# Local-window attention and two wide products on one core: contexts split straight from PSUM, a reordered head, and q/k blocks of 736 columns

## The chip, the cores and the metric

The kernel runs on one core of one Trainium2 chip. The metric is device time in microseconds (us) of one execution; smaller is better. The engines are TensorE (PE, with its weight loads shown as PEld), VectorE (DVE), ScalarE (ACT), GpSimd (POOL) and SyncE (SP), which here issues all the transfers. Everything is 32-bit floating point. A product of full precision is made of three passes, high by high, high by low and low by high, so each operand exists as a "high" tile and a "low" tile.

## The reference

```python
# 4 batches, 8 heads, 512 local and 32 global positions, head width 64, window 32
s_g   = scale * q_g @ concat(k_g, k_l).T;  out_g = softmax(s_g) @ concat(v_g, v_l)
s_ll  = where(|i - j| <= 32, scale * q_l @ k_l.T, -1e9)
s_l   = concat(scale * q_l @ k_g.T, s_ll); out_l = softmax(s_l) @ concat(v_g, v_l)
x = concat(out_g, out_l) as (2176 tokens, 512)
x = max(x @ w1, x @ w2, x @ w3) @ w_out          # inner width 768
x = softplus(x @ w_in) @ w_out2                  # inner width 2048
```

## The kernel before, in words

The order on each engine is written out by hand: one stream of attention steps (`att_stream`), one stream that turns the weights from their stored 64-bit form into high and low tiles (`dec_stream`, four DVE operations, an ACT copy and a POOL subtraction for each of 24 weight tiles), and loops over the products that step through both.

**Attention.** There are 32 groups k: batch, half of the sequence (hf), pair of heads (pr). A group's block `kq` holds the queries of four blocks of 64 positions (u = 0 to 3) and the keys. `s1` makes the scores of the four query blocks and two heads, eight matmuls of 64 rows and 64 columns of weights each (L142), into the one PSUM tile `ps`, and DVE masks them into `s` and takes the row extremes (L148). `s1e` is the Exp on ACT (L155), `s1f` the reciprocal on DVE and the scaling on POOL, `s2` five transposes into `pw` and `pg` (L211, L212), `s2e` their evictions to `pwt` and `pgt` (L223 and L225 on ACT, L227 on DVE), `s3` the context product `po` (L238, L242), `s3h` and `s3l` its eviction. Iteration k runs `s1(k)`, `s3` of group k-3 and `s2` of group k-2. The scores of the global queries are made by `s1g` (tile `psg`, copied to `gsc`), softmaxed by `gsoft` in three steps (L195; L197; L199 to L201), transposed by `g2` (`pb`, `pa`), and multiplied by `g3` (`pog`, evicted by `g3e`).

**Units.** Eight groups of four make eight units u of 256 columns (288 with the global rows, for odd u). The first product (`up`, tile `pu`, L516 to L518) of unit u reads the context as `xh` and `xl`. For units 0 and 1 `s3h` and `s3l` split `po` from PSUM into them; for units 2 to 7 `s3h` copies `po` to `xo` and sends it to the DRAM tile `xd`, and `load_x` fetches it (`xr`) and splits it. The maximum `m` of three `pu` tiles is split by `split_h` into `hh` and `hl`, which the second product (`down`, tile `pd`, L562 to L564) reads. The PSUM tiles `po`, `pw`, `pg`, `psg`, `pa`, `pb`, `pog`, `pu` and `pd` share five buffers of the pool `pm`.

**The head** is the stretch of iterations k < 12 (`KS`), where attention runs ahead and the products of unit 0 begin at k = 7. Then follow the products of units 0 and 1 (until the last of `w1`, `w2`, `w3` is decoded they use each weight as it comes), `down(0)`, `down(1)`, and so on. From about 160 us on TensorE works nearly without a gap to the end.

Of the kernel before, what the change touches and what calls it, by code (L numbers as in the profile page):

```python
# [21 lines left out]
def body(ctx, tc, kq, vw, vb, qg, w1, w2, w3, w_out, w2_in, w2_out, out):  # L22
# [8 lines left out]
    HLP = 3  # L31
# [16 lines left out]
    mask = const.tile([128, 3, 160], F32, name="mask")  # L48

    def setup():  # L50
        g = nc.gpsimd
        g.memset(mask[:, 0, :], 0.0)
        for hh in range(2):
            m = mask[64 * hh:64 * hh + 64, 0, 0:128]
# [4 lines left out]
        g.memset(mask[0:64, 1, 0:32], NEG)  # L59
        g.memset(mask[64:128, 2, 96:128], NEG)  # L60
# [3 lines left out]
    raw, qgs, vbs = {}, {}, {}  # L64

    def load_kq(k):
# [6 lines left out]
        st[k] = {"q": t[:, 0:256].rearrange("p (u n) -> p u n", n=64), "kT": t[:, 256:896].rearrange("p (u n) -> p u n", n=160)}  # L73
# [17 lines left out]
    xs = {}  # L91
    gs = {}
# [6 lines left out]
    def split_x(u, ks, ns, p):  # L99
        xh, xl = xs[u] if u in xs else new_x(u)  # L100
# [3 lines left out]
    def load_x(u):  # L104
        n = 256 + 32 * (u % 2)
        xh, xl = new_x(u)
        xr = []
        for k in range(4):
            xr.append(hp.tile([128, 288], F32, tag="m", name="xr")[:, 0:n])
            nc.sync.dma_start(out=xr[k], in_=xd[u][:, k, 0:n])  # L110
        yield
        for k in range(4):
            nc.scalar.activation(xh[:, k, 0:n], xr[k], AF.Copy)
            (nc.gpsimd if XLP > u else nc.vector).tensor_tensor(xl[:, k, 0:n], xr[k], xh[:, k, 0:n].bitcast(F32), op=ALU.subtract)
            yield
# [11 lines left out]
    def s1(k, w):  # L127
        b, hf, pr = groups[k]
        g = st[k]
        if w == 0:  # L130
            if k < KL:
                g["s"] = wp.tile([128, 4, 160], F32, tag="w", name="s")
            else:
                g["s"] = at.tile([128, 4, 160], F32, tag="s", name="s", bufs=3)
# [11 lines left out]
        for i in range(2):  # L146
            x = 2 * w + i
            nc.vector.tensor_tensor_reduce(out=s[:, x, :], in0=ps[:, i, :], in1=mask[:, mi, :], scale=-scale, scalar=BIG,  # L148
                                           op0=ALU.add, op1=ALU.min, accum_out=g["nm"][:, x:x + 1])

    def s1e(k, i):
        g = st[k]
        s = g["s"]
        for u in (2 * i, 2 * i + 1):
            nc.scalar.activation(s[:, u, :], s[:, u, :], AF.Exp, scale=-1.0, bias=g["nm"][:, u:u + 1], accum_out=g["sm"][:, u:u + 1])  # L155

    def s1f(k):
# [6 lines left out]
        nc.gpsimd.tensor_tensor(s[:, :, 0:128], s[:, :, 0:128], rs.unsqueeze(2).to_broadcast([128, 4, 128]), op=ALU.mult)  # L164
        nc.gpsimd.tensor_tensor(sg, s[:, :, 128:160], rs.unsqueeze(2).to_broadcast([128, 4, 32]), op=ALU.mult)
        g["sg"] = sg

    def s1g(k):
# [3 lines left out]
        ps = ptile([128, 288], "psg")  # L172
        ks = [st[k - 1]["kT"], g["kT"]]
        r = raw[b, hf, s]
        for j in range(2):
            kk = ks[j].rearrange("p (a c) n -> p a c n", c=2)
            nc.tensor.matmul(ps[64 * j:64 * j + 64, 0:256], lhsT=qgs[b][:, pr - 1 + j, :], rhs=kk[:, :, 0, 0:128], start=True, stop=True)
# [3 lines left out]
        else:  # L181
            for j in range(2):
                nc.tensor.matmul(ps[64 * j:64 * j + 64, 256:288], lhsT=qgs[b][:, pr - 1 + j, :], rhs=ks[j][:, 3, 64:96], start=True, stop=True)
# [20 lines left out]
    def s2(k):  # L204
# [5 lines left out]
        for x in range(4):  # L210
            nc.tensor.transpose(pw[:, 128 * x:128 * x + 128], g["s"][:, x, 0:128], ident)  # L211
# [1199 lines left out]
```

## Time and profile before

| what | value |
|---|---|
| median of 3 runs | 780.06 us (778.52 to 780.24) |
| the profiled execution's own time | 780.84 us |
| its span, first to last instruction | 779.1 us |
| TensorE busy | 750.6 us (96%) |
| VectorE busy | 571.7 us (73%) |
| ScalarE busy | 373.4 us (48%) |
| GpSimd busy | 250.8 us (32%) |
| mean granted TensorE clock | 0.998 |

All times of rows are counted from the span's start. 1.74 us of the execution's time lie outside the span.

### The profile page before, as it was taken

The numbers are of one execution on the slowest core, as the hardware profiler recorded it, in microseconds if no ns is written. First come the engines' busy times: TensorE is split into PE (matmuls) and PEld (weight loads), VectorE is DVE, ScalarE is ACT, GpSimd is POOL, SyncE is SP. The second block draws the span as 40 slices with busy tenths as digits, with TensorE's granted clock in tenths as the row PEclk, the third lists the DMA queues.
The fourth block names the chain that finished last, engine by engine and source line by source line (L and its number), as shares of the span: only waits on it lengthen the run. The fifth ranks groups of instructions, "written<-read, shape, count | busy, mean of one in ns | idle before, by whom it ended". The sixth has DMA issues, their size and how long they took to land.

```text
span 779.1 us, 18128 instructions
## 1 busy us (share of the span) xinstructions
PE 750.6 (96%) x6984; PEld 722.0 (93%) x6984; DVE 571.7 (73%) x1438; ACT 373.4 (48%) x955; POOL 250.8 (32%) x240
## 2 busy tenths in 40 slices
PE   5779999999999999999999999999999999999998
PEld 3669998898999999999999999999999999999998
DVE  5978985677786686693991465544686889999996
ACT  5865445654554652233432455533554444444443
POOL 4544441112211210161960488943872000000000
PEclk9999999999999999999999999999999999999999
DMA  8938225777767746578010455445539923444432
GB/s 332 363 128 312 105 84 184 261 283 248 257 213 250 251 170 203 197 267 295 12 42 28 151 179 200 138 159 185 175 132 370 378 93 109 136 136 135 137 95 82
DMA packets 80742, 145.62 MB, mean 187 GB/s; under 512 B 10128, under 2 KB 45840, under 8 KB 80656
## 3 DMA queue, kind: packets, MB, share of 16 engines
q1 hardware_dynamic: 80656, 144.47, 53.9%
q8 instruction: 55, 0.90, 0.5%
q14 instruction: 31, 0.25, 0.1%
HBM read 98.63 MB, written 45.81 MB: 185 GB/s over the span
## 4 chain that ended last, share of the span: by engine, by line
PE 77%; DVE 8%; DMA 4%; ACT 4%; issue 3%; POOL 3%; SPq 0%; POOLq 0%; ACTq 0%; DVEq 0%
PE pu L516 8%; PE pu L518 8%; PE pu L517 8%; PE z L1216 6%; PE z L1040 6%; PE z L1041 6%; PE z L1039 6%; PE z L1215 6%; PE z L1214 6%; DMA raw<-in_w_dram 3%; PE pog L294 2%; PE ps L142 2%; PE pd L562 2%; PE pd L563 2%; PE po L238 2%
## 5 line engine op out<-in xcount | busy, mean ns | idle before, releaser
L516 PE MATMUL pu<-xh,w 128*128 128x256 f32 (+1 forms) x576 | 169.2, 294 | 0.5 <-DVE m L530 0.5
L518 PE MATMUL pu<-xh,w 128*128 128x256 f32 (+1 forms) x576 | 166.5, 289 | 0.8 <-POOL w L453 0.8
L517 PE MATMUL pu<-xl,w 128*128 128x256 f32 (+1 forms) x576 | 166.7, 289 | 0.0
L1216 PE MATMUL z<-v,oo 128*128 128x256 f32 x480 | 136.8, 285 | 0.5 <-DVE oo L1210 0.4
L1215 PE MATMUL z<-v,oo 128*128 128x256 f32 x480 | 135.6, 282 | 0.0
L1214 PE MATMUL z<-v,oo 128*128 128x256 f32 x480 | 135.1, 282 | 0.0
L1040 PE MATMUL z<-o,wi 128*128 128x272 f32 x448 | 129.0, 288 | 1.6 <-POOL o L652 1.6
L1041 PE MATMUL z<-o,wi 128*128 128x272 f32 x448 | 129.1, 288 | 0.0
L1039 PE MATMUL z<-o,wi 128*128 128x272 f32 x448 | 128.7, 287 | 0.1
L516 PEld LDWEIGHTS pu<-xh,w 128*128 128x128 f32 x576 | 109.2, 190 | 3.4 <-issue 1.5
L518 PEld LDWEIGHTS pu<-xh,w 128*128 128x128 f32 x576 | 108.8, 189 | 1.2 <-POOL w L453 1.2
L517 PEld LDWEIGHTS pu<-xl,w 128*128 128x128 f32 x576 | 109.0, 189 | 0.0
L1209 ACT ACTIVATE oo<-sm 128x640 fp32r<-128x640 f32 (+1 forms) x72 | 49.8, 692 | 93.4 <-DVE sm L1204 87.5
L1216 PEld LDWEIGHTS z<-v,oo 128*128 128x128 f32 x480 | 90.8, 189 | 1.3 <-DVE oo L1210 1.0
L1214 PEld LDWEIGHTS z<-v,oo 128*128 128x128 f32 x480 | 91.3, 190 | 0.1
L1215 PEld LDWEIGHTS z<-v,oo 128*128 128x128 f32 x480 | 90.9, 189 | 0.0
L164 POOL TENSOR_TENSOR s<-s,rs 128x512 f32<-128x512 f32 x32 | 34.5, 1079 | 161.3 <-DVE rs L162 94.4
L1040 PEld LDWEIGHTS z<-o,wi 128*128 128x128 f32 x448 | 84.1, 188 | 2.2 <-POOL o L652 2.2
L1039 PEld LDWEIGHTS z<-o,wi 128*128 128x128 f32 x448 | 84.5, 189 | 0.3 <-DVE h L1061 0.3
L1041 PEld LDWEIGHTS z<-o,wi 128*128 128x128 f32 x448 | 84.2, 188 | 0.0
L1210 DVE TENSOR_TENSOR oo<-sm,oo 128x640 fp32r<-128x640 f32 (+1 forms) x72 | 55.0, 764 | 16.5 <-ACT oo L1209 12.8
L652 POOL TENSOR_TENSOR o<-ot,o 128x544 fp32r<-128x544 f32 x36 | 50.9, 1426 | 45.8 <-DVE h L1082 33.8
(161 smaller groups left out, 1641.8 us busy)
## 6 DMA issues: line engine op xcount, KB each, us to landing
gd<-a SPq DMA_DIRECT2D x32, 544.0 KB, 3.1
gl<-gd SPq DMA_DIRECT2D x32, 512.0 KB, 7.1
kq<-in_kq_dram SPq DMA_DIRECT2D x31, 448.0 KB, 5.9
raw<-in_w_out_dram SPq DMA_DIRECT2D x22, 512.0 KB, 4.6
raw<-in_w_dram SPq DMA_DIRECT2D x18, 512.0 KB, 7.6
vt<-in_vw_dram SPq DMA_DIRECT2D x16, 512.0 KB, 6.5
raw<-in_w_in_dram SPq DMA_DIRECT2D x16, 512.0 KB, 5.3
ot<-od SPq DMA_DIRECT2D x24, 272.0 KB, 3.1
```

The lines of the kernel that those rows point to most:

```text
L516: nc.tensor.matmul(p, lhsT=w[:, 0, k], rhs=xh[:, k, 0:n], start=(k == 0), stop=False)
L517: nc.tensor.matmul(p, lhsT=w[:, 0, k], rhs=xl[:, k, 0:n], start=False, stop=False)
L518: nc.tensor.matmul(p, lhsT=w[:, 1, k], rhs=xh[:, k, 0:n], start=False, stop=(k == 3))
L652: nc.gpsimd.tensor_tensor(w[:, 1], src, w[:, 0].bitcast(F32), op=ALU.subtract)
L1039: nc.tensor.matmul(z, lhsT=w[:, 0, k], rhs=x[:, 0, k], start=st and k == 0, stop=False, skip_group_check=True)
L1040: nc.tensor.matmul(z, lhsT=w[:, 0, k], rhs=x[:, 1, k], start=False, stop=False, skip_group_check=True)
L1041: nc.tensor.matmul(z, lhsT=w[:, 1, k], rhs=x[:, 0, k], start=False, stop=sp and k == 1, skip_group_check=True)
L1209: nc.scalar.activation(oh[:, a:b], src, AF.Copy)
L1210: nc.vector.tensor_tensor(ol[:, a:b], src, oh[:, a:b].bitcast(F32), op=ALU.subtract)
L1214: nc.tensor.matmul(p, lhsT=oh[:, a], rhs=w[:, 0], start=st, stop=False, skip_group_check=True)
L1215: nc.tensor.matmul(p, lhsT=oh[:, a], rhs=w[:, 1], start=False, stop=False, skip_group_check=True)
L1216: nc.tensor.matmul(p, lhsT=ol[:, a], rhs=w[:, 0], start=False, stop=sp, skip_group_check=True)
```

## The change

It has four parts.

1. `kq` blocks have 736 columns for 896 (368 KB for 448 KB). Instead of four copies of 128 keys and 32 global keys, a block holds global keys, a run of 192 keys, global keys, another run of 192, global keys; query blocks u = 0 and 1 read two stretches of 160 columns that share a run, as u = 2 and 3 do. With this a query block's half of the PSUM rows is chosen by u // 2 and its columns by u % 2 (before: the other way round), and mask, `s`, `po` and `pwt` are indexed to match.
2. Context tiles of units 2 and 3 are also split straight from PSUM when the tiles `xh`, `xl` of the unit two before have been read by all of its `up` products (`here`, `freed`, `direct`); `load_x` fetches only the parts that were not.
3. In the head: `flush()` evicts the pending `pu` before each `s1`; in iterations with a `g2` the evictions `s3h` and `s2e` come before the Exp; the global softmax begins one iteration earlier; `psg` and `pog` share one PSUM buffer in odd iterations.
4. The low halves `hl` of unit 0 are all made on POOL (before: three of six; the others on DVE); the split of unit 1's `m` comes after all of `down(0)`, and 6 steps of attention (before: 4) stand between that and `down(1)`.

```diff
-    HLP = 3
+    HLP = 6
...
-        t = ld.tile([128, 896], F32, tag="kq", name="kq", bufs=5)
+        t = ld.tile([128, 736], F32, tag="kq", name="kq", bufs=5)
         if k == 0:
-            nc.sync.dma_start(out=t[:, 0:576], in_=kq[k][:, 0:576])
-            nc.sync.dma_start(out=t[:, 576:896], in_=kq[k][:, 576:896])
+            nc.sync.dma_start(out=t[:, 0:512], in_=kq[k][:, 0:512])
+            nc.sync.dma_start(out=t[:, 512:736], in_=kq[k][:, 512:736])
...
     def load_x(u):
-        n = 256 + 32 * (u % 2)
-        xh, xl = new_x(u)
+        xh, xl = xs[u] if u in xs else new_x(u)
+        parts = []
+        for k in range(4):
+            x = [(u, k) not in direct, u % 2 and (u, "g" + str(k // 2)) not in direct]
+            if any(x):
+                parts.append((k, slice(0 if x[0] else 256, 288 if x[1] else 256)))
...
             for u in range(4):
                 for i in range(2):
                     h = slice(64 * i, 64 * i + 64)
-                    r0, c0 = 64 * (u % 2), 160 * (u // 2)
-                    nc.tensor.matmul(g["ps"][r0:r0 + 64, i, c0:c0 + 160], lhsT=g["q"][h, u, :], rhs=g["kT"][h, u, :], start=True, stop=True)
+                    r0, c0, k0 = 64 * (u // 2), 160 * (u % 2), (0, 96, 224, 320)[u]
+                    nc.tensor.matmul(g["ps"][r0:r0 + 64, i, c0:c0 + 160], lhsT=g["q"][h, u, :], rhs=g["kT"][h, k0:k0 + 160], start=True, stop=True)
...
+    def here(u, x):
+        if u not in xs and u - 2 in freed:
+            new_x(u)
+        if u in xs:
+            direct.add((u, x))
+        return u in xs
...
-        if 2 * b + hf < 2:
-            if hf not in xs:
-                new_x(hf)
-            nc.scalar.activation(xs[hf][0][:, pr:pr + 1, 0:256], po.unsqueeze(1), AF.Copy)
+        if here(2 * b + hf, pr):
+            nc.scalar.activation(xs[2 * b + hf][0][:, pr:pr + 1, 0:256], po.unsqueeze(1), AF.Copy)
             return
...
             if k < KS:
+                if True:
+                    flush()
                 s1(k, 0)
                 s1(k, 1)
...
+                joint = ptile([128, 352], "psg") if late and k % 2 == 1 else None
                 for c in late:
-                    g3(*c)
+                    g3(*c, None if joint is None else joint[:, 288:352])
+                if gq and q3 is not None:
+                    s3h(q3)
+                if gq and q2 is not None:
+                    s2e(q2)
                 s1e(k, 0)
                 s1e(k, 1)
-                if q3 is not None:
+                if not (gq) and q3 is not None:
                     s3h(q3)
...
                 if gq:
                     g2(*gq)
-                elif gpend:
+                if gpend:
                     soft = gsoft()
                     next(soft)
...
-        if by_row:
-            for f in range(6):
-                split_h(u + 1, f)
         for j in range(2):
             o = hp.tile([128, 288], F32, tag="m", name="o")[:, 0:n]
...
-        AS = 4
+        AS = 6
...
             if u == 0:
+                for f in range(6):
...
+                    split_h(1, f)
                 for _ in range(AS):
                     step()
```

Three places in the order of the engines, before and after. ACT in iteration k = 8 of the head: `s` is the score tile of group 8 (Exp), `pg` and `pw` are the transposes of group 6, `pu` the first product of unit 0, and `pa` one of the transposes of the global softmax. Before:

```order
L452 ACTIVATE w<-tmp 128x512
L155 ACTIVATE s,sm<-s,nm 128x160 x4
L252 ACTIVATE xh<-po 128x256
L223 ACTIVATE pgt<-pg 128x128
L225 ACTIVATE pwt<-pw 128x512
L527 ACTIVATE m<-pu 128x256
L458 ACTIVATE tmp<-raw 128x512
L282 ACTIVATE gt<-pa 128x384
```

After:

```order
L476 ACTIVATE w<-tmp 128x512
L551 ACTIVATE m<-pu 128x256
L267 ACTIVATE xh<-po 128x256
L233 ACTIVATE pgt<-pg 128x128
L235 ACTIVATE pwt<-pw 128x512
L161 ACTIVATE s,sm<-s,nm 128x160 x4
L482 ACTIVATE tmp<-raw 128x512
L207 ACTIVATE gsc,gsm<-gsc,gnm 128x544
L297 ACTIVATE gt<-pa 128x384
```

The four evictions of PSUM tiles stand ahead of the Exp now, and the Exp of the second global softmax (`gsc`) has come into this iteration from the next.

DVE in iterations 9 and 10: the end of that global softmax. Before, it stands in iteration 10, right behind that iteration's scores (`rs` is the reciprocal of group 9) and ahead of the eviction of `pb`, its transpose:

```order
L161 TENSOR_SCALAR rs<-sm 128x4
L162 RECIPROCAL rs<-rs 128x4
L199 TENSOR_SCALAR gsm<-gsm 128x1
L200 RECIPROCAL gsm<-gsm 128x1
L201 TENSOR_SCALAR gsc<-gsc,gsm 128x544
L530 TENSOR_TENSOR m<-m,pu 128x256
L472 TENSOR_SCALAR tmp<-tmp 128x512
```

After, it stands in iteration 9, ahead of the eviction of `pw`:

```order
L167 TENSOR_SCALAR rs<-sm 128x4
L168 RECIPROCAL rs<-rs 128x4
L209 TENSOR_SCALAR gsm<-gsm 128x1
L210 RECIPROCAL gsm<-gsm 128x1
L211 TENSOR_SCALAR gsc<-gsc,gsm 128x544
L237 COPY pwt<-pw 128x512
L508 SCALAR_TENSOR_TENSOR tmp<-raw,t_724 128x512
```

It moved one iteration ahead, and the eviction of `pw` waits behind it.

DVE at the end of `down(0)`: `hl` are the six low halves of unit 1, `s,nm<-ps` the masking of a group's scores (four pieces, each with a second row for its extremes), `tmp` words of the next weights. Before, the splits stand ahead of the first of the four pieces:

```order
L227 COPY pwt<-pw 128x512
L161 TENSOR_SCALAR rs<-sm 128x4
L162 RECIPROCAL rs<-rs 128x4
L632 TENSOR_SCALAR tmp<-tmp 128x512
L634 TENSOR_SCALAR tmp<-tmp 128x512
L548 TENSOR_TENSOR hl<-m,hh 128x288 x6
L148 ISA s,nm<-ps,mask 128x160
```

After, the same four pieces follow the two operations on `tmp`, and these rows come behind the last piece:

```order
L154 ISA s,nm<-ps,mask 128x160
L154 ISA nm 128x1
L278 TENSOR_TENSOR xl<-po,xh 128x256
L661 SCALAR_TENSOR_TENSOR tmp<-raw,tmp 128x512
L665 SCALAR_TENSOR_TENSOR tmp<-raw,tmp 128x512
L205 TENSOR_REDUCE gnm<-gsc 128x1
L653 TENSOR_SCALAR tmp<-tmp 128x512
L655 TENSOR_SCALAR tmp<-tmp 128x512
L572 TENSOR_TENSOR hl<-m,hh 128x288 x6
```

The six splits moved behind the scores and behind five operations on words and the global softmax, and a split of a context tile (`xl<-po`) came in.

## Rows read from the trace of the kernel before

**Rows 1.** The page, busy time of each engine (us, share of the span, instructions).
```profile
PE 750.6 (96%) x6984; PEld 722.0 (93%) x6984; DVE 571.7 (73%) x1438; ACT 373.4 (48%) x955; POOL 250.8 (32%) x240
```

**Rows 2.** Waits of TensorE over the whole span: total us, times, longest.
```profile
PE ps L142 <- DMA kq<-in_kq_dram: 5.5, 2, 3.8
PE po L238 <- ACT pgt L223: 3.8, 5, 1.0
...
PE pog L294 <- DVE pwt L227: 1.3, 2, 0.7
...
PE pu L518 <- POOL w L453: 0.8, 2, 0.6
```

**Rows 3.** Busy time of each engine in four stretches.
```profile
core 0: us, PE busy (x) PEld busy (x) DVE busy (x) ACT busy (x) POOL busy (x), PEclk, DMA share, GB/s
...
10.40:17.20 6.80, 6.80 (x68) 4.71 (x69) 6.00 (x25) 4.75 (x19) 3.23 (x5) 1.00 1.03 412
...
12.90:41.00 28.10, 21.28 (x309) 16.46 (x309) 26.62 (x102) 23.05 (x87) 16.71 (x19) 0.99 0.91 352
41.00:67.00 26.00, 23.41 (x305) 20.25 (x305) 20.09 (x64) 15.97 (x52) 10.89 (x13) 0.95 0.48 169
67.70:111.00 43.30, 42.47 (x350) 41.67 (x350) 39.91 (x77) 19.96 (x40) 18.86 (x15) 1.00 0.39 148
```

**Rows 4.** Timeline, TensorE's wait for the first global queries.
```profile
10.40 1.12 PE L177 MATMUL psg<-kq,qg 128*64 128x256 f32 x4 [2.23 <-DMA qg<-in_qg_dram]
```

**Rows 5.** Timeline of ACT and PE in iteration 8, and a stretch's busy times and clock.
```profile
38.74 0.43 ACT L155 ACTIVATE s<-s,nm 128x160 f32<-128x160 f32 x1 [0.93 <-DVE nm L148]
...
40.67 0.26 ACT L223 ACTIVATE pgt<-pg 128x128 f32<-128x128 f32 x1
...
40.98 1.12 PE L275 MATMUL pa<-ident,gsc 128*128 128x128 f32 x4 [2.76 <-ACT pgt L223]
...
40.38:43.79 3.41, 2.81 (x13) 2.78 (x14) 2.13 (x6) 3.33 (x10) 1.34 (x3) 0.50 0.00 0
```

**Rows 6.** Timeline of DVE and PE in iteration 10.
```profile
56.63 1.15 DVE L201 TENSOR_SCALAR gsc<-gsc,gsm 128x544 f32<-128x544 f32 x1
...
57.92 0.29 PE L272 MATMUL pb<-ident,gsc 128*96 128x128 f32 x1 [1.24 <-DVE gsc L201]
```

**Rows 7.** Timeline of the decoding stretch: low halves on DVE and POOL, PE's last wait.
```profile
83.52 0.43 DVE L548 TENSOR_TENSOR hl<-m,hh 128x256 fp32r<-128x256 f32 x1 [0.49 <-ACT hh L545]
...
65.49 0.73 POOL L548 TENSOR_TENSOR hl<-m,hh 128x256 fp32r<-128x256 f32 x1 [0.31 <-ACT hh L545]
...
95.49 0.39 PE L518 MATMUL pu<-xh,w 128*128 128x256 f32 x1 [0.58 <-POOL w L453]
```

**Rows 8.** Timeline of DVE and PE at the end of `down(0)`.
```profile
128.09 2.29 DVE L548 TENSOR_TENSOR hl<-m,hh 128x288 fp32r<-128x288 f32 x6
130.30 0.32 DVE L148 CUSTOM_DVE_ANT_0 s<-ps,mask 128x160 f32<-128x160 f32 x1
...
131.46 0.37 PE L142 MATMUL ps<-kq 64*64 64x160 f32 x4 [1.73 <-issue]
```

**Rows 9.** Timeline of ACT and PE in `down(1)`.
```profile
142.40 0.75 ACT L113 ACTIVATE xh<-xr 128x256 fp32r<-128x256 f32 x2 [3.17 <-DMA xr<-xd]
...
145.04 0.39 ACT L186 ACTIVATE gsc<-psg 128x288 f32<-128x288 f32 x1
...
145.48 0.41 PE L562 MATMUL pd<-hh,w 128*128 128x288 f32 x1 [1.58 <-ACT gsc L186]
```

**Rows 10.** Score matmuls (L142) of iteration 9: records; PE, PEld records in a stretch.
```profile
L142 PE MATMUL ps<-kq x16: 296/296/347, 45.7 to 46.2; 64*64 64x160 f32 x16
...
45.66:45.71 0.05, 0.03 (x4) 0.03 (x4) 1.00 0.00 0
...
45.86:45.89 0.03, 0.03 (x8) 0.03 (x8) 1.00 0.00 0
...
45.99:46.03 0.04, 0.04 (x12) 0.04 (x8) 1.00 0.00 0
```

More of the change, by code (lines that the diff above doesn't have):

```diff
@@ L47, in body @@
     ident = const.tile([128, 128], F32, name="ident")
-    mask = const.tile([128, 3, 160], F32, name="mask")
+    mask = const.tile([128, 3, 192], F32, name="mask")
     def setup():
@@ L99, in split_x @@
     def split_x(u, ks, ns, p):
-        xh, xl = xs[u] if u in xs else new_x(u)
+        xh, xl = xs[u]
         nc.scalar.activation(xh[:, ks, ns], p, AF.Copy)
@@ L104, in load_x @@
     def load_x(u):
-        n = 256 + 32 * (u % 2)
-        xh, xl = new_x(u)
+        xh, xl = xs[u] if u in xs else new_x(u)
[4 more added lines that the diff above has]
+                parts.append((k, slice(0 if x[0] else 256, 288 if x[1] else 256)))
         xr = []
-        for k in range(4):
-            xr.append(hp.tile([128, 288], F32, tag="m", name="xr")[:, 0:n])
-            nc.sync.dma_start(out=xr[k], in_=xd[u][:, k, 0:n])
+        for k, c in parts:
+            xr.append(hp.tile([128, 288], F32, tag="m", name="xr")[:, 0:c.stop - c.start])
+            nc.sync.dma_start(out=xr[-1], in_=xd[u][:, k, c])
         yield
-        for k in range(4):
-            nc.scalar.activation(xh[:, k, 0:n], xr[k], AF.Copy)
-            (nc.gpsimd if XLP > u else nc.vector).tensor_tensor(xl[:, k, 0:n], xr[k], xh[:, k, 0:n].bitcast(F32), op=ALU.subtract)
+        for (k, c), r in zip(parts, xr):
+            nc.scalar.activation(xh[:, k, c], r, AF.Copy)
+            nc.vector.tensor_tensor(xl[:, k, c], r, xh[:, k, c].bitcast(F32), op=ALU.subtract)
             yield
@@ L171, in s1g @@
         g = st[k]
-        ps = ptile([128, 288], "psg")
+        ps = ptile([128, 288], "psg") if joint is None else joint
         ks = [st[k - 1]["kT"], g["kT"]]
@@ L175, in s1g @@
         for j in range(2):
[L176 to L177 removed]
+            kk = ks[j][:, 32:480].rearrange("p (c n) -> p c n", n=224)[:, :, 0:128]
+            nc.tensor.matmul(ps[64 * j:64 * j + 64, 0:256], lhsT=qgs[b][:, pr - 1 + j, :], rhs=kk, start=True, stop=True)
         if hf == 0:
@@ L182, in s1g @@
             for j in range(2):
-                nc.tensor.matmul(ps[64 * j:64 * j + 64, 256:288], lhsT=qgs[b][:, pr - 1 + j, :], rhs=ks[j][:, 3, 64:96], start=True, stop=True)
+                nc.tensor.matmul(ps[64 * j:64 * j + 64, 256:288], lhsT=qgs[b][:, pr - 1 + j, :], rhs=ks[j][:, 384:416], start=True, stop=True)
             t = gs[b, s]["t"]
@@ L237, in s3 @@
             for i in range(2):
-                nc.tensor.matmul(po[64 * i:64 * i + 64, 2 * w:2 * w + 2, :], lhsT=vbs[b, s][:, e, w, 64 * i:64 * i + 64], rhs=g["pgt"],
+                nc.tensor.matmul(po[64 * i:64 * i + 64, w:w + 3:2, :], lhsT=vbs[b, s][:, e, w, 64 * i:64 * i + 64], rhs=g["pgt"],
                                  start=(w == 0), stop=False, skip_group_check=True)
@@ L288, in g3 @@
         vs = [(v0, 0, 128), (v0, 2, 128), (v1, 0, 128), (v1, 2, 64), (v1, 3, 96)]
-        po = ptile([128, 2, 32], "pog")
+        if joint is None:
+            joint = ptile([128, 64], "pog")
+        po = joint.rearrange("p (a n) -> p a n", n=32)
         for e in range(2):
@@ L350, in att_stream @@
                 next(soft, None)
-                if q2 is not None:
+                if not (gq) and q2 is not None:
                     s2e(q2)
@@ L363, in att_stream @@
                 if k % 2 == 1:
-                    s1g(k)
+                    s1g(k, None if joint is None else joint[:, 0:288])
                 for c in late:
@@ L867, in slot @@
             pos[u] += 1
+            if pos[u] == 18:
+                freed.add(u)
         def ready(u):
@@ L956, in body @@
             ldx = itertools.chain.from_iterable(load_x(v) for v in loads_x)
-            if loads_x:
-                next(ldx)
+            next(ldx, None)
             for c in range(4):
@@ L971, in body @@
             if u == 0:
+                for f in range(6):
+                    if f >= 1:
+                        for _ in range(0):
+                            step()
+                    split_h(1, f)
                 for _ in range(AS):
```

55 lines of the change are left out of this document (31 added, 24 removed).

## Prediction

> **What bounds the kernel now.** I read the page first: TensorE is busy for 750.6 us of a span of 779.1 [rows 1]. The change neither adds nor takes away a matmul, so there are 28.5 us to win, TensorE's idle time, and what it runs at half clock. The waits of TensorE say where that idle time is: nearly all of it is ahead of 150 us, in the start (5.5 us for q/k blocks, 3.8 us for evictions) and then in single waits [rows 2]. Three stretches of the busy times tell what is behind them [rows 3]. From 12.9 to 41 us DVE is the bound (26.6 of 28.1 us busy) and TensorE waits at every group. From 41 to 67 us neither is (TensorE 23.4 and DVE 20.1 of 26): the engines wait for each other in turn. From 67.7 to 111 us TensorE is busy for 42.5 of 43.3 us, and DVE, which decodes the weights that TensorE reads, for 39.9. So a gain made before 67 us arrives only if the decoding moves forward with it; this is the point to check. Behind 150 us TensorE has no idle time worth counting until the second half, which the change does not touch, so what is won before then stays won.
>
> **The change part by part.** *Smaller q/k blocks.* A block is 160 of 896 columns smaller, 80 KB. Up to 17 us the DMA is full (share 1.03, 412 GB/s [rows 3]) and TensorE and DVE wait for landings, the last time TensorE at 10.40 us for the global queries [rows 4]. Ahead of these three blocks are in the queue, 240 KB, 0.6 us at that rate; by 17 us five, 1.0 us. I take 0.8 us; the bounds are 0 (the waits end with something else) and nine blocks, 1.8 us. All later saving of bytes lies under a TensorE that does not wait for DMA, and is worth nothing here.
>
> *Evictions ahead of the Exp.* In iteration 8 the transposes `pa` wait 2.76 us for ACT's `pgt` [rows 5]. ACT is at the Exp of group 8, for which it waited until 38.74 us, and the eviction of group 6 stands behind that. After the change the order on ACT is `m`, `xh`, `pgt`, `pwt`, Exp: all four have their inputs before 38.2 us, so `pa` follows `pb` directly. The wait goes but for 0.1 us: 2.7. Behind the wait the clock was granted at 0.50, the lower of the two levels, from 40.38 to 43.79 us; TensorE was busy for 2.81 us of it [rows 5], work of 1.4 us at the full clock. Without the gap it should not fall: 1.3. What is late next is the Exp, by the 1.2 us that four evictions take; it feeds the transposes of group 8 in iteration 10, some 10 us later.
>
> *Softmax one iteration earlier, shared buffer.* `pb` waits 1.24 us for the end of the second global softmax on DVE [rows 6], which takes 1.15 us there. It moves to iteration 9, where DVE has room (5.9 us idle in this stretch), so the wait is gone: 1.2. It now stands ahead of the eviction of `pw`, which is then 1.5 us later; `pog` waited for just that one, 1.3 us in two places [rows 2]. With the shared buffer `pog` takes one that a `pu` left and that `flush()` empties before the scores: 1.3, bounds 0 and 1.3. These four terms make 6.5 us by 67 us, on TensorE.
>
> *Does the decoding follow?* DVE's place in the order is tied to TensorE by the scores and by `m`. Laying the new DVE order over the durations of the old rows from iteration 8 on, I find DVE's scores of iteration 11 some 6 us earlier too, with the same decoding behind it, because it fills the 5.9 us in which it was idle. The weights' transfers follow, since SP issues them behind `pog` and `psg`. *Low halves on POOL:* between 67.7 us and the last weight of the first product DVE makes two of them, alike, 0.43 us each with a wait of 0.49 us for ACT in front [rows 7]: 1.8 us less for the decoding. On POOL one takes 0.73 us, in gaps between its weights; `down(0)` needs them only 15 us later. So the decoding gains more than TensorE, and its waits for weights, the last at 95.49 us, 0.8 us in all [rows 2, 7], go: 0.8.
>
> *Split of unit 1 moved.* At 131.46 us TensorE waits 1.73 us for the buffer of the scores, because DVE does six `hl` (2.29 us) ahead of reading the scores [rows 8]. Behind the scores they are out of its way: 1.7. But then they come some 4 us later, since five more operations stand ahead of them, while `down(1)` reads the first of them just behind two groups' worth of attention matmuls. TensorE may wait for `hl` there instead, between 0 and the whole 1.7; the splits then run at 0.38 us each (2.29 for six), faster than `down(1)` uses them, so only the first can be late. I put 0.3 on it: 1.4.
>
> *Unit 2 from PSUM.* ACT stands 3.17 us for the landing of `xr`, and its eviction of `gsc` comes late for `pd`, 1.58 us [rows 9]. Of the four fetches one is left, of a part stored long before. The wait goes: 1.5. For unit 3 no wait was there: 0.
>
> The sum is 0.8 + 2.7 + 1.3 + 1.2 + 1.3 + 0.8 + 1.4 + 1.5 = 11.0 us. 780.84 us for the execution profiled gives 769.8; it lies 0.8 above the median of the runs, so I forecast **769.5**.
>
> *The score matmuls.* They are the part whose price the trace does not show. The eight matmuls of a group leave 16 records, two each, and four of them run at a time: four begin within 0.05 us, four more by 45.89 us and four more by 46.03, a round each 0.135 us [rows 10]. These are the four places that the loop visits in turn (two heads by two halves of the PSUM rows). After the change the halves are chosen by u // 2, so four matmuls in a row go to two places, then four to the other two. If TensorE looks far enough ahead, all four places work at once as before: 0. If not, a group takes up to 8 rounds instead of 4: four pairs of matmuls with two records each, 7 if only the change of halves overlaps. 24 of 32 groups (k from 8 on) lie where TensorE is dense, so each further round costs 24 x 0.135 = 3.25 us, and the bounds are 0 and 13. I take 0, because a far look is already needed: the fourth matmul starts ahead of the first one's second record.
>
> The Trainium skill (TensorE: Matmul & The Clock Gate, Part 3, on packing small matmuls) speaks against this: matmuls begin and end strictly in program order, and only weight loads overlap where the row groups differ. Taken so, a matmul for a place that is busy holds up all behind it, seven rounds for a group, and the sum would be 779.3. The rows with four starts in 0.05 us, out of matmuls of two records each, do not agree with the strict rule, so it stays a rival.
>
> **The rivals.** *Tile order.* As above, with 5, 6, 7 and 8 rounds: 772.8, 776.0, 779.3, 782.5. The last is the case on the other side, slower; it takes more than 3.7 further rounds, where the 11 us and 0.2% of the time are eaten up.
>
> *The decoding does not follow.* Then the 6.5 us are given back at 95 us, where TensorE waits for the last weight, and what is left is 1.4 and 1.5 behind, and up to 1.8 by the low halves: 775 to 777. For it: DVE is 92% busy there. Against it: its idle time before 67 us.
>
> *Buffers held longer.* A context that is split from PSUM is read by ACT and then DVE, where ACT alone was enough; seven groups (k = 9 to 15). If TensorE waits 0.3 to 0.7 us at each: 771.5 to 774.5. For it: five buffers and a DVE that is busy. Against it: for units 0 and 1 it was so already, and no wait for it is among the rows.
>
> **How the numbers follow.** The forecast has 0.55 (its own range 767.5 to 771.5), tile order 0.25 (0.10, 0.07, 0.05, 0.03), buffers 0.10, decoding 0.07, something else 0.03. The range from 767 to 776.5 leaves out 7 and 8 rounds, a third of the decoding case and the low end, under 0.2. A measurement of this kernel can tell 0.2% (1.6 us) from no change: faster is all but 7 and 8 rounds, something else and the tail of the decoding case, 0.88; the same 0.06; slower 0.06.
>
> **What would show it.** In the profile after: no wait of `pa` and no granted clock of 0.5 around 40 us; no waits of `pb`, `pog`, `pu` and of the scores at the end of `down(0)`; ACT no longer standing for `xr`. `down(0)` should begin 8 us earlier. The score matmuls of a group should still end 0.6 us after their start; if they take 0.8 to 1.1, it is tile order. Wrong it would be if a new wait of TensorE stood between 41 and 111 us for `w`, or for `hl` in `down(1)`.

## The result and the profile after

The changed kernel takes **769.32 us** (median of 4 runs, 768.74 to 769.55); the kernel before took 779.82 us beside it (778.52 to 780.24). The ratio is 0.9867 with a 95% interval of 0.985 to 0.9884: 10.5 us less. The profiled execution takes 769.23 us with a span of 767.5 us, 11.6 us less than that of before.

The page's line of busy times. TensorE does the same work (6984 instructions) in a span that has 17.7 us without it, for 28.5 before [rows 1]:

```profile
PE 749.8 (98%) x6984; PEld 722.0 (94%) x6984; DVE 568.9 (74%) x1435; ACT 371.9 (48%) x950; POOL 252.5 (33%) x243
```

The waits of TensorE over the whole span (total us, times, longest). The waits of `pa`, `pb` and `pog` [rows 2, 5, 6] are no longer among them; `pd` for `hh` (in `down(1)`) is new; the one for `hl` is at 340 us. At the start the waits for landings fall from 7.7 us (`kq` 5.5, `qg` 2.2) to 4.5, but 2.4 us more of waits of the scores come in their place (`nm`, and `pg`, for 0.5 before), so that 1.0 us is left at iteration 8:

```profile
PE ps L148 <- DMA kq<-in_kq_dram: 3.7, 1, 3.7
PE po L248 <- ACT pgt L233: 2.8, 4, 1.0
...
PE ps L148 <- PE pg L222: 1.6, 3, 0.6
PE ps L148 <- DVE nm L154: 1.3, 1, 1.3
PE pd L586 <- ACT hh L569: 0.9, 1, 0.9
PE psg L187 <- DMA qg<-in_qg_dram: 0.8, 1, 0.8
...
PE pu L540 <- ACT pgt L233: 0.4, 1, 0.4
PE pd L587 <- DVE hl L572: 0.3, 1, 0.3
...
PE pu L542 <- POOL w L477: 0.2, 1, 0.2
```

The same stretches as in [rows 3] and [rows 5]. TensorE is now busy for 25.6 of the 26 us from 41 to 67, and its clock is full where it was 0.50:

```profile
core 0: us, PE busy (x) PEld busy (x) DVE busy (x) ACT busy (x) POOL busy (x), PEclk, DMA share, GB/s
12.90:41.00 28.10, 24.54 (x343) 20.02 (x347) 26.50 (x97) 24.57 (x90) 16.63 (x19) 1.00 0.82 307
41.00:67.00 26.00, 25.60 (x330) 22.60 (x323) 24.49 (x73) 17.27 (x55) 14.44 (x15) 1.00 0.67 244
67.70:111.00 43.30, 42.93 (x388) 41.79 (x387) 38.09 (x88) 20.91 (x48) 22.25 (x20) 1.00 0.30 118
40.38:43.79 3.41, 3.20 (x60) 2.50 (x58) 3.27 (x10) 2.00 (x5) 1.28 (x1) 1.00 0.00 0
```

Iteration 8, timelines of ACT and of TensorE. The evictions `m`, `xh`, `pgt` and `pwt` run from 36.67 us on, the Exp comes behind them, and `pa` follows `pb` without a wait:

```profile
36.67 0.36 ACT L551 ACTIVATE m<-pu 128x256 f32<-128x256 f32 x1
36.94 0.38 ACT L267 ACTIVATE xh<-po 128x256 fp32r<-128x256 f32 x1
37.20 0.28 ACT L233 ACTIVATE pgt<-pg 128x128 f32<-128x128 f32 x1
37.36 0.61 ACT L235 ACTIVATE pwt<-pw 128x512 f32<-128x512 f32 x1
37.84 0.45 ACT L161 ACTIVATE s<-s,nm 128x160 f32<-128x160 f32 x1
...
36.93 0.27 PE L287 MATMUL pb<-ident,gsc 128*96 128x128 f32 x1
37.09 0.65 PE L290 MATMUL pa<-ident,gsc 128*128 128x128 f32 x4
37.53 0.39 PE L540 MATMUL pu<-xh,w 128*128 128x256 f32 x1
```

Where the time comes from is read by setting the starts of the same matmuls side by side (from the timelines of TensorE; at each of these places the same work has been done in both):

| TensorE begins | before, us | after, us | ahead by |
|---|---|---|---|
| scores of iteration 8 | 35.59 | 34.56 | 1.0 |
| scores of iteration 9 | 45.68 | 40.58 | 5.1 |
| scores of iteration 11 | 61.50 | 54.56 | 6.9 |
| last third of unit 0's first product | 74.49 | 67.29 | 7.2 |
| last third of unit 1's first product | 103.18 | 94.61 | 8.6 |
| `down(0)` | 117.64 | 109.69 | 8.0 |
| first product of unit 5 | 317.22 | 306.99 | 10.2 |
| first product of unit 6 | 356.88 | 345.88 | 11.0 |
| second product of unit 6 | 412.04 | 400.28 | 11.8 |

Behind that the distance changes by 0.2 us at most.

### The profile page after: what moved, and what is told of

It is laid out like the page before. It is cut to its first block, busy times and chain, and to the rows that moved or that the text cites. A ratio compares the mean times of both kernels' runs of the same rounds, so it can differ in the third digit from the quotient of the medians.

```text
span 767.5 us, 18081 instructions
## 1 busy us (share of the span) xinstructions
PE 749.8 (98%) x6984; PEld 722.0 (94%) x6984; DVE 568.9 (74%) x1435; ACT 371.9 (48%) x950; POOL 252.5 (33%) x243
## 4 chain that ended last, share of the span: by engine, by line
PE 77%; DVE 10%; ACT 4%; issue 3%; POOL 3%; DMA 2%; SPq 1%; DVEq 0%; POOLq 0%; ACTq 0%
PE pu L540 8%; PE pu L542 8%; PE pu L541 8%; PE z L1244 6%; PE z L1068 6%; PE z L1069 6%; PE z L1067 6%; PE z L1243 6%; PE z L1242 6%; PE ps L148 2%; PE pd L587 2%; PE pw L221 2%; PE po L248 2%; PE pd L588 2%; PE pd L586 2%
## 5 line engine op out<-in xcount | busy, mean ns | idle before, releaser
L1238 DVE TENSOR_TENSOR oo<-sm,oo 128x640 fp32r<-128x640 f32 (+1 forms) x72 | 55.1, 765 | 16.5 <-ACT oo L1237 12.8
L673 POOL TENSOR_TENSOR o<-ot,o 128x544 fp32r<-128x544 f32 x36 | 50.9, 1426 | 45.8 <-DMA ot<-od 33.8
```

The lines of the kernel that those rows point to most:

```text
L673: nc.gpsimd.tensor_tensor(w[:, 1], src, w[:, 0].bitcast(F32), op=ALU.subtract)
L1238: nc.vector.tensor_tensor(ol[:, a:b], src, oh[:, a:b].bitcast(F32), op=ALU.subtract)
```

## The experiments

The theory: the prediction's terms (evictions, softmax, decoding, split of unit 1, unit 2) each take away the wait that it names, and they add up. Its rivals are the prediction's (the order of the score matmuls costs rounds; the decoding does not follow; buffers are held longer) and that a term took away what another one took away too. Kernels 1, 9 and 11 put parts together or alone, the others undo one part of the changed kernel (2 to 6) or alter it (7, 8, 10, 12). The kernel before was timed beside them: 779.87 us (1 to 4), 780.12 (5 to 8) and 780.21 (9 to 12).

**1. The head alone**, on the kernel before.

```diff
             if k < KS:
+                flush()
                 s1(k, 0)
...
+                if gq and q3 is not None:
+                    s3h(q3)
+                if gq and q2 is not None:
+                    s2e(q2)
                 s1e(k, 0)
...
-                elif gpend:
+                if gpend:
```

(and the shared buffer `joint` as in the change)

> The kernel before with part 3 alone (head reordered); q/k blocks stay at 896 columns, three low halves of unit 0 stay on DVE, units 2 and 3 go by DRAM, the split of unit 1 stays in down(0). Theory (the decoding moves forward with the head, as TensorE's gain is DVE's gain too): the 2.8 us wait of pa, the clock of 0.5 behind it, and the waits of pb and pog go, the first product of unit 0's second maximum starts 5.5 to 6 us earlier, and this is still there at down(0): 773 to 774.5, ratio 0.991 to 0.993. Rival (the decoding does not follow without the low halves on POOL): TensorE waits for w between 80 and 96 us for 3 us or more, where it waited 0.8; down(0) starts at most 3 us earlier: 777 to 778.5, ratio 0.996 to 0.998.

773.23 us (772.59 to 773.93), ratio 0.9918 (0.9903 to 0.9933). Ahead by 0.6 us at the scores of iteration 8, 6.5 at iteration 11, 6.8 at the last third of unit 0 and still 6.8 at `down(0)`, with TensorE's waits for `w` at 0.8 us as before. The decoding follows by itself: this rival is out. Two of the runs took 772.6 us with a mean granted clock of 1.0, the other two 773.8 and 773.9 with 0.998.

**2. Evictions behind the Exp again.**

```diff
-                if gq and q3 is not None:
-                    s3h(q3)
-                if gq and q2 is not None:
-                    s2e(q2)
                 s1e(k, 0)
                 s1e(k, 1)
-                if not (gq) and q3 is not None:
+                if q3 is not None:
                     s3h(q3)
...
-                if not (gq) and q2 is not None:
+                if q2 is not None:
                     s2e(q2)
```

> The changed kernel with the evictions of po, pw and pg behind the Exp again in the iterations with a transpose of the global softmax; all else stays. Theory (these evictions were the whole reason for the 2.8 us wait and for the clock of 0.5 behind it): pa waits 2 to 3 us for pgt near 39 us, the granted clock falls to 0.5 for some 3 us, and the time is 772.5 to 773.5. Rival (the earlier eviction of the pending maximum by the flush had already taken the wait away): no fall of the clock, pa waits under 1 us, 769.3 to 770.

772.09 us (770.44 to 772.88), ratio 0.9896 (0.988 to 0.9913). The wait is back, with `pu` behind `pa` as the one that waits (the flush had freed `pa`'s buffer), for the same `pgt`, and the clock falls behind it. Waits of TensorE from 34 to 60 us, and the busy times from 39.8 to 43 us (columns as above):

```profile
PE pu L536 <- ACT pgt L233: 2.6, 2, 2.2
```

```profile
39.80:43.00 3.20, 3.20 (x15) 3.20 (x16) 2.59 (x7) 3.20 (x7) 0.66 (x2) 0.50 0.00 0
```

In this execution (772.88 us) scores of iteration 9 start 9.9 us behind those of iteration 8, for 6.0 in the changed kernel: 3.8 us for the wait and the clock. Its median is below what was expected, by 0.4 us; the profiled one is the slowest of the four. The fastest, 770.44 us, is the only one with a mean granted clock of 1.0; the others have 0.997 or 0.998.

**12. The same with the wait filled.** This one repeats the last transpose of `pa` twenty times; nothing that is read changes.

```diff
             nc.tensor.transpose(pa[0:n, 128 * i:128 * i + 128], t[:, o:o + n], ident)
+        if (b, s) == (0, 0):
+            for _ in range(20):
+                nc.tensor.transpose(pa[0:64, 384:512], t[:, 384:448], ident)
```

> The kernel of experiment 2 (evictions behind the Exp) with 20 more transposes of the same piece into the same place of pa behind the first pa, which fill TensorE's wait there; they repeat work and change nothing that is read. Theory (the clock falls because TensorE stood still for the 2.2 us): the granted clock stays at 1.00 at 40 to 43 us, the scores of iteration 9 start 1.2 to 1.6 us earlier after those of iteration 8 than in experiment 2, and the time is 770.6 to 771.2. Rival (the clock falls for another reason, or its fall costs nothing): the interval between these scores and the time are those of experiment 2, 9.9 us and 772.1, or more.

770.87 us (770.54 to 771.25), ratio 0.988 (0.9854 to 0.9906). The 20 transposes take 2.35 us from 37.09 to 39.44, a little more than the wait, the clock stays at 1.00, and the interval from scores to scores is 8.4 us, 1.4 less than in 2:

```profile
39.80:43.00 3.20, 3.20 (x40) 3.05 (x38) 2.62 (x7) 2.81 (x7) 0.87 (x1) 1.00 0.00 0
```

So of the 3.8 us 1.4 are the clock's, and with TensorE kept at work the clock did not fall. By the medians it is 1.2 of 2.8 us.

**3. Three low halves on DVE.**

```diff
-    HLP = 6
+    HLP = 3
```

> The changed kernel with three of the six low halves of unit 0 back on DVE. Theory (DVE bounds the decoding between 67 and 95 us, so two low halves with their wait for ACT make it later): waits of TensorE for w come back, 0.5 to 1.5 us in all, 770.0 to 770.8. Rival (the decoding has slack in the changed kernel): no wait for w over 0.2 us and 769.1 to 769.6.

770.08 us (769.62 to 770.18), ratio 0.9876 (0.9862 to 0.9891), 0.8 above the changed kernel. The waits of TensorE from 67 to 111 us have the old one again, where the changed kernel has none for `w` (its 0.2 us lie ahead of 67):

```profile
PE pu L542 <- POOL w L477: 0.8, 2, 0.6
```

The profile says more than that wait: between the last third of unit 0 and that of unit 1 it loses 1.4 us. The stretch takes 28.7 us in all four profiles with three low halves on DVE and 27.3 in all ten without. The theory holds; DVE sets the pace there.

**4. Blocks of 896 columns** of which 736 are read.

```diff
-        t = ld.tile([128, 736], F32, tag="kq", name="kq", bufs=5)
+        t = ld.tile([128, 896], F32, tag="kq", name="kq", bufs=5)
...
-            nc.sync.dma_start(out=t[:, 512:736], in_=kq[k][:, 512:736])
+            nc.sync.dma_start(out=t[:, 576:896], in_=kq[k][:, 576:896])
```

> The changed kernel with q/k blocks padded to 896 columns that nothing reads beyond 736: only bytes and landings change. Theory (the start is bound by landings): scores of iterations 2 and 3 start later by some 1 us and the shift stays to the end, 770.1 to 770.5. Rival (the start was already bound by DVE and the chain of evictions): shift under 0.3 us at iteration 4, 769.2 to 769.6.

769.41 us (768.84 to 769.73), ratio 0.9868 (0.9853 to 0.9883): no difference that can be measured. Yet in its profile the scores of iteration 8 start at 35.27 us for 34.56. One execution does not settle it, since the landings at the start vary; over all profiles of this study it is 35.0 to 35.6 us in the four with 896 columns (mean 35.2) and 33.8 to 35.8 in the ten with 736 (mean 34.5). So 0.7 us are likely at the start; in this execution they were gone by the first product of unit 6, where TensorE had waited for `hl` in the changed kernel (below) and did not here.

**5. Units 2 and 3 by DRAM.**

```diff
     def here(u, x):
-        if u not in xs and u - 2 in freed:
+        if u > 1:
+            return False
+        if u not in xs:
             new_x(u)
-        if u in xs:
-            direct.add((u, x))
-        return u in xs
+        direct.add((u, x))
+        return True
```

> The changed kernel with the contexts of units 2 and 3 sent to DRAM and fetched again, as before; all else stays. Theory (ACT stands for the landing of the fetched tile in down(1) and TensorE behind it): ACT waits some 3 us for xr, TensorE waits 1.5 us in down(1) and the time is 770.5 to 771. Rival (the fetch is hidden once the split of unit 1 and six steps stand ahead of down(1)): TensorE's waits in down(1) stay under 0.5 us and the time is 769.1 to 769.7. A third: the direct split costs buffers, and without it the time is under 769.

768.73 us (767.96 to 769.44), ratio 0.9859 (0.9843 to 0.9874). The third case: by the medians 0.6 us less than the changed kernel, by the intervals not to be told from it. ACT no longer stands for the fetch, which was issued from 127.26 us on; in its timeline the split of `xr` follows an eviction at once:

```profile
131.31 0.69 ACT L592 ACTIVATE o<-pd 128x288 f32<-128x288 f32 x2
131.89 0.72 ACT L119 ACTIVATE xh<-xr 128x256 fp32r<-128x256 f32 x2
```

And the wait of 0.37 us at 104.00 us (`pu` for `pgt`, above) is gone. From the last third of unit 1 to the scores of iteration 13 this kernel gains 0.6 us on the changed one; over all profiles that stretch takes 12.2 us in the five without part 2 and 12.8 in the nine with it, so the cost goes with this part. The likely reason, not tested by itself, is the second reader of `po`: here ACT's copy of it ends at 102.97 us and `pu` starts at 103.02, while in the changed kernel DVE's split of it ends at 103.83 and `pu` starts at 104.00.

**6. The split of unit 1 back in `down(0)`**, 4 steps.

```diff
+        if by_row:
+            for f in range(6):
+                split_h(u + 1, f)
         for j in range(2):
             o = hp.tile([128, 288], F32, tag="m", name="o")[:, 0:n]
...
-        AS = 6
+        AS = 4
...
-                for f in range(6):
...
-                    split_h(1, f)
```

> The changed kernel with the split of unit 1's maximum back ahead of the last evictions of down(0), and 4 steps of attention ahead of down(1). Theory (the move takes 1.7 us of waiting for the score buffer away, and gives 0.9 to 1.3 back as the wait of down(1) for the first high and low half, which come behind the Exp on ACT): the wait for scores is back, the one for hh is gone, 769.6 to 770.1. Rival (the move is worth its whole 1.4): 770.5 to 771.

770.79 us (769.83 to 771.46), ratio 0.9881 (0.9864 to 0.9899), 1.5 above the changed kernel: the rival's time. The wait for `hh` goes, but the one for the scores is longer than before, 2.3 us, and the clock falls behind it to 0.57 (124 to 128 us). Its length follows a weight block: DVE's six `hl` stand behind two operations on words that ACT copied from it, and ACT comes to it 3.4, 3.7, 4.0 and 4.4 us after its fetch was issued in the profiles of before, 1, 6 and 11, where the wait is 1.7, 2.0, 2.3 and 2.7 us. The one run with a mean clock of 1.0 took 769.83 us, 0.5 above the changed kernel, and the other three, with 0.997 to 0.999, 770.68 to 771.46: a good part of the 1.5 goes with the clock. The waits from 110 to 150 us are this one:

```profile
PE ps L148 <- issue: 2.3, 1, 2.3
```

**7. Only the first split early.**

```diff
+        if by_row:
+            for f in range(1):
+                split_h(u + 1, f)
...
-                for f in range(6):
...
+                for f in range(1, 6):
```

> The changed kernel with only the first of the six splits of unit 1 put back ahead of the last evictions of down(0). Theory (the wait at the start of down(1) is for the first high and low half alone, since the other splits are made faster than they are used): the wait of 0.94 for hh and 0.3 for hl goes, the scores wait for DVE's one operation of 0.4 us at most; 768.2 to 768.8. Rival (the second split is then as late as the first was): 769.0 to 769.4.

768.94 us (768.65 to 769.5), ratio 0.9863 (0.9848 to 0.9877). The wait of 0.9 us for `hh` is gone, but the scores now wait for 0.5 us behind the early split. By the profiles 0.4 us are gained at `down(1)`; the time is between the two expectations and not to be told from the changed kernel's.

**8. The score matmuls of one place in a row.**

```diff
-            for u in range(4):
-                for i in range(2):
+            for u, i in ((0, 0), (1, 0), (0, 1), (1, 1), (2, 0), (3, 0), (2, 1), (3, 1)):
+                if True:
```

> The changed kernel with the eight score matmuls of a group in an order in which two in a row always go to the same of the four places. Theory (each place of 64 rows and 64 columns takes its own matmuls as they come, and TensorE looks far enough ahead to start the other places): a group takes 0.77 to 0.85 us and the time is 769.1 to 770.5. Rival (matmuls start strictly in program order): 12 to 13 rounds of 0.135 us for 4, a group takes 1.9 to 2.0 us, and 24 dense groups give some 28 us: 795 to 800. Between them: a look-ahead of two or three matmuls, 8 rounds, a group takes 1.3 us, 781 to 784.

768.91 us (768.64 to 769.37), ratio 0.9862 (0.9847 to 0.9877). The theory, without a remainder: the group takes 0.79 us in this kernel, as it does in the changed one. The starts say which matmuls begin first. The first four records begin 0, 7, 13 and 20 ns into the group in the kernel before, 0, 7, 27 and 34 ns in the changed one, and 0, 13, 26 and 40 ns here. The records do not name the matmul; at the 7 ns from one matmul to the next of the kernel before, that fits the 1st to 4th in program order, then the 1st, 2nd, 5th and 6th, then the 1st, 3rd, 5th and 7th: each time the first one of each of the four places. Timeline of TensorE in iteration 9:

```profile
40.45 0.79 PE L148 MATMUL ps<-kq 64*64 64x160 f32 x16
```

**9. Experiment 5 with 4 steps.**

```diff
-        AS = 6
+        AS = 4
```

> The kernel of experiment 5 (changed kernel, units 2 and 3 by DRAM) with 4 steps of attention between down(0) and down(1) instead of 6; the split of unit 1 stays moved. Theory (the wait for the fetched context was taken away by the two further steps, which give the stores, the fetch and its landing more time ahead of ACT's reading): ACT stands for xr again, TensorE waits 1 to 1.6 us in down(1), 769.7 to 770.4. Rival (moving the split alone gave that time): no wait for it and 768.5 to 769.2.

770.32 us (769.92 to 771.02), ratio 0.9875 (0.9844 to 0.9905). The time is the theory's, the reason is not. ACT stands for `xr` for only 0.6 us, and TensorE not at all for it; the wait at the start of `down(1)` has grown from 1.0 to 1.7 us, since less attention work covers the making of `hh`. Those 0.7 us are not all of the 1.6 between the medians; by the first product of unit 5 its profile is 1.0 us behind that of 5. Waits from 110 to 150 us:

```profile
PE pd L587 <- ACT hh L570: 1.7, 1, 1.7
```

So moving the split took most of the wait for the fetch away (3.17 us of ACT before [rows 9]), and the two further steps cover `hh`.

**11. Part 2 alone**, on the kernel before (`here`, `freed`, `direct` and `load_x` as in the change).

```diff
-        if 2 * b + hf < 2:
+        if here(2 * b + hf, pr):
...
-        if b == 0:
-            split_x(1, slice(2 * s, 2 * s + 2), slice(256, 288), po)
+        if here(2 * b + 1, "g" + str(s)):
+            split_x(2 * b + 1, slice(2 * s, 2 * s + 2), slice(256, 288), po)
```

> The kernel before with part 2 alone (contexts of units 2 and 3 split from PSUM). Theory (as predicted: the fetch is what ACT stands for in down(1), and TensorE waits 1.58 us behind it): that wait is gone, 778.2 to 778.8. Rival (what the fetch gave up is lost again, as PSUM buffers are held for a second reader): 779.3 to 780.3, with new waits of TensorE behind po between 100 and 150 us.

779.22 us (777.72 to 782.21), ratio 0.9987 (0.9972 to 1.0002): unclear, and between the two. The profile agrees with the rival's reason in part. The wait for `xr` in `down(1)` (1.58 us [rows 9]) is gone; 0.4 us stand behind `pgt`, and the one for the scores has grown from 1.73 [rows 8] to 2.7 us, with the clock's fall behind it. The growth goes with the later weight block (experiment 6); that part 2 is its cause is not shown. Waits from 100 to 150 us:

```profile
PE ps L147 <- issue: 2.7, 1, 2.7
PE pu L526 <- ACT pgt L228: 0.4, 1, 0.4
```

From the last third of unit 1 to the first product of unit 2 it loses 1.1 us on the kernel before, 0.6 of it ahead of the scores of iteration 13.

**10. Without part 2, first split early** (the diffs of 5 and 7).

> The changed kernel without its part 2 (units 2 and 3 by DRAM, as in experiment 5) and with the first split of unit 1 early (as in experiment 7), as a version that may be better than both. If both gains are real and add up, 0.6 and 0.4 us below 769.3: 768.1 to 768.6. If one of them was chance, 768.7 to 769.2.

768.19 us (767.19 to 770.05), ratio 0.9849 (0.9824 to 0.9874), the lowest of all. The expectation is met in the median, but its interval holds the changed kernel's ratio, so that it is better is not shown. What its profile shows is that these are all the waits of TensorE from 34 to 410 us:

```profile
PE ps L148 <- PE pg L222: 0.5, 1, 0.5
PE po L248 <- ACT pgt L233: 0.4, 1, 0.4
PE psg L312 <- DVE m L555: 0.2, 1, 0.2
PE pu L543 <- POOL w L478: 0.2, 1, 0.2
```

## Why the prediction was right, and where it was not

769.5 us was forecast and 769.32 measured; taken off the profiled execution the sum gives 769.8, off the median 769.1, and the forecast lies between them. By the profiled executions 11.0 us were summed and 11.6 found. The mechanism holds for the head and the decoding; that the size agrees so well is in part luck, as several errors cancel.

| term | forecast, us | found between the two profiles, us |
|---|---|---|
| smaller blocks | 0.8 | 1.0 |
| evictions ahead of the Exp, and the clock | 2.7 + 1.3 | 4.1 |
| softmax earlier, shared buffer | 1.2 + 1.3 | 2.1 |
| low halves on POOL | 0.8 | 1.4 |
| split of unit 1 moved, unit 2 from PSUM | 1.4 + 1.5 | 2.3, less 0.6 lost ahead of `down(0)` |
| after unit 5's first product | 0 | 1.4 |

*Right, with an experiment behind it.* **Evictions:** undone, they cost 3.8 us in one profile and 2.8 by the medians, and the filled wait shows that 1.4 (by the medians 1.2) of it is the clock (1.3 forecast). **The head's gain arrives:** experiment 1 has 6.8 us at 67 us and at `down(0)`, and the changed kernel begins `down(0)` 8.0 us earlier, as was said. The rival "the decoding does not follow" is out, and this without the low halves on POOL: the step that DVE gains its own idle time back was enough. **Tile order:** out. The group takes 0.79 us, and with two matmuls in a row for one place still 0.79 (experiment 8). The prediction took 0 because four matmuls began together, and by the starts above a place does take its own matmuls ahead of the order in the program. Its sign, an end 0.6 us after the start, was misread: the group took 0.77 us before the change, too. The Trainium skill (TensorE: Matmul & The Clock Gate, Part 3) states that matmuls begin and end strictly in program order; these runs do not agree, as strict order would make experiment 8's groups 12 to 13 rounds of 0.135 us [rows 10], some 1.7 us.

*Off in size.* **Low halves on POOL** were put at 0.8 us, the waits for `w`; by the profiles the stretch is 1.4 us shorter. The term that was mis-sized is the cost of a wait: the two waits of experiment 3 there, 0.83 us, cost 1.37, as each one cost about 0.27 us more than its row (see the last section). By the medians of experiment 3 it is 0.8; in the profiles 0.5 us of it are covered behind 317 us, where the changed kernel waits for `hl` (below) and experiment 3 does not. **Smaller blocks:** the profiles suggest 0.7 us at iteration 8 (experiment 4); no time shows it.

Then the two sizes that were put on **the split of unit 1**: the new wait in `down(1)` was taken at 0.3 us and is 0.94, for `hh`; `hl` is not late. The step that failed is that only the five operations on DVE were counted ahead of the splits. The first one has its high half made on ACT, and there it stands behind the Exp of the attention and of the global softmax. Timelines of ACT and TensorE in the changed kernel:

```profile
124.71 0.74 ACT L207 ACTIVATE gsc<-gsc,gnm 128x544 f32<-128x544 f32 x1
...
125.44 0.76 ACT L569 ACTIVATE hh<-m 128x288 fp32r<-128x288 f32 x2
...
125.92 0.40 PE L586 MATMUL pd<-hh,w 128*128 128x288 f32 x1 [0.94 <-ACT hh L569]
```

The whole term measures 1.5 us by the medians of experiment 6 for 1.4 forecast; in its profile the wait that it takes away is 2.3 us and not 1.73, as the weight block came later, with the clock's fall behind it. From the start of `down(0)` to the first product of unit 5, where the work is the same in all, the profiles have 199.5 to 199.6 us with neither the moved split nor part 2 (before, 1), 200.1 with part 2 and the old split (6, 11, both with the longer wait and the clock's fall), 197.6 with the moved split and six steps alone (5), and 197.3 with both (the changed kernel). So the move, with its two further steps, is worth 2.0 us alone, and 2.8 beside part 2, of which the later block and the clock are a part.

*Wrong.* **Unit 2 from PSUM** was put at 1.5 us. The wait for the fetch is indeed gone, but with the split moved it is gone when the fetch is made, too (experiments 5 and 9). The step that failed is to price a wait of the old order for one edit, when another edit of the same change moves ACT's work around it: ACT comes to the fetched tile 3.0 us after the issue of its fetch before, and 4.6 us after it in experiment 5. What part 2 adds ahead of `down(0)` is 0.6 us more between 95 and 107 us, in each profile that has it. Beside the moved split it gains 0.3 us behind that (197.3 for 197.6), so by the profiles its term is a loss of some 0.3 us; the medians do not tell it from nothing, there or in experiment 11. The 0.6 us fit the rival "buffers held longer", at one place and smaller than it was put (2 to 5 us over seven groups).

**What was not forecast** are 1.4 us behind 317 us, in a part that the prediction said the change does not touch. In the profile of before TensorE waits there twice, 1.04 us for `hl` and 0.50 for `m` (at 392 us); after, once, 0.26 us for `hl`. By the length of the stretches (last section) that is 0.8 us for each. Timeline before, then after, in the second product of unit 5:

```profile
349.63 1.34 POOL L652 TENSOR_TENSOR vc<-qv,vc 128x512 fp32r<-128x512 f32 x1
349.87 1.42 DVE L548 TENSOR_TENSOR hl<-m,hh 128x288 fp32r<-128x288 f32 x1
351.33 0.40 PE L563 MATMUL pd<-hl,w 128*128 128x288 f32 x1 [1.04 <-DVE hl L548]
```

```profile
312.81 0.46 DVE L572 TENSOR_TENSOR hl<-m,hh 128x288 fp32r<-128x288 f32 x1
...
338.60 1.36 POOL L673 TENSOR_TENSOR vc<-qv,vc 128x512 fp32r<-128x512 f32 x1
338.84 1.44 DVE L572 TENSOR_TENSOR hl<-m,hh 128x288 fp32r<-128x288 f32 x1
...
340.33 0.40 PE L587 MATMUL pd<-hl,w 128*128 128x288 f32 x1 [0.26 <-DVE hl L572]
```

DVE's operation is as slow in both; TensorE comes 0.8 us less early for it after the change. This wait is between 0 and 1.0 us in the profiles of the experiments, without a rule that goes with one part. What sets it is left open, so these 1.4 us are luck as far as the prediction goes. It also hides a part of what is won or lost ahead of it, which is how the 0.7 us of experiment 4 disappeared.

So the sum of 11.0 stands beside 11.6 because 1.4 us came that were not foreseen and the low halves brought 0.6 more, while the split and unit 2 together brought 1.2 less than their 2.9; the other terms differ by 0.4 or less each.

## What to carry to other kernels

- A wait shown in a profile may be removed by more than one edit of a change: price each with the others already made, above all where they move work on the same engine's queue, and count the second reader that a "direct" path puts on a buffer (here the profiles show more lost than gained by it).
- On an engine whose order the program writes out, put the evictions that another engine's next buffer hangs on ahead of long work that nobody waits for; here that was worth 3.8 us in one profile and 2.8 by the medians, of which 1.4 and 1.2 were the clock behind the wait.
- A gain in an early stage can arrive at the end, as it did here, if the engine that bounds the next stage was itself idle in the early one; read that from its busy time there before fearing that it is given back.

## What the runs showed of the hardware that was not expected

**The clock does not always fall behind the same wait.** Part 2 alone has the same wait of `pa` as before, 2.76 us at 40.41 us, and the clock stays at 1.00 in the stretch where it was 0.50 [rows 5]; scores follow scores there in 8.9 us for 10.1. Later in the same execution it falls, behind the 2.7 us for the scores. Timeline of TensorE, and busy times of two stretches of that kernel:

```profile
40.41 0.66 PE L285 MATMUL pa<-ident,gsc 128*128 128x128 f32 x4 [2.76 <-ACT pgt L228]
```

```profile
40.38:43.79 3.41, 3.38 (x28) 3.29 (x28) 2.09 (x7) 2.74 (x6) 1.34 (x2) 1.00 0.01 3
131.20:135.00 3.80, 3.71 (x46) 3.24 (x46) 3.63 (x11) 3.04 (x12) 0.27 (x1) 0.60 0.89 269
```

So a term for the clock is one that an execution may or may not have. The mean clock of the single runs agrees: in experiments 1, 2, 6 and 9 the runs at 1.0 are the fastest (772.6 us for 773.8 and 773.9 in experiment 1). All four runs of the changed kernel are at 1.0, and none of the 31 of the kernel before beside the experiments is above 0.998, so the wider spread of that kernel (778.0 to 784.7 us there) is likely in part the clock. What decides whether it falls is open.

**One subtraction on DVE, 0.46 or 1.44 us.** The rows above show the same operation on the same shape: 0.46 us at 312.81, with POOL idle, and 1.44 us at 338.84 beside POOL's split `vc`.

**Four places of TensorE's array keep their own order.** 64-row, 64-column matmuls to one place, issued two in a row, cost the group nothing: 0.79 us for eight in either order.

**A wait among dense matmuls cost more than its row.** The matmuls of the products start about 0.13 us apart while each record lasts 0.28 to 0.29 us, and the profile counts a wait from the end of the one before; the first one behind a wait lasts 0.39 to 0.40 us. So the wait of 1.04 us for `hl` made the stretch from the second product of unit 5 to the first of unit 6 10.88 us long, and the one of 0.26 us 10.10, where it is 9.6 in the eight profiles without that wait. In all six profiles that have it (0.19 to 1.04 us) it costs 0.26 or 0.27 us more than its row. The 0.50 us for `m` cost 0.76 (55.16 us, for 54.40 after the change, from there to the second product of unit 6), and the two waits of experiment 3 for `w` 0.27 each beyond their rows: a price read from the table of waits was too low by that much for each of these.
